# Differences of key groups with chained scores, a fifth block of maxima, a one-piece turn, and a list schedule for phase 1

## The chip, the cores and the metric

The kernel runs on one core of a Trainium2 chip. The metric is the device time of one execution in microseconds; lower is better.

## The reference

Attention over 8 batches and 8 heads with pairs of query rows pooled, and then a token and channel mixer on its output:

```
q_pool = q.reshape(B, H, S // 2, 2, D).mean(axis=3)       # S = 1152, D = 64
scores = scale * (q_pool @ k.T)                           # 576 x 1152 per head
scores = scores - max(scores, axis=-1)
attn = exp(scores);  attn = attn / (sum(attn, -1) + 1e-9)
x = attn @ v                                              # 576 x 64 per head, heads side by side: 576 x 512
theta = x @ w_theta;  zr = x * cos(theta);  zi = x * sin(theta)
y = w_tok_r @ zr + w_tok_i @ zi                           # over the 576 tokens
u = x + y;  out = u + relu(u @ w_ch)
```

q, k and w_theta come with large values, so the float32 scores are formed as a sum of products of high and low parts.

## The kernel before

**Phase 1, attention.** The 64 heads are worked two at a time: 32 pairs, one head in partitions 0 to 63 and one in 64 to 127. For each pair SyncE's queue loads q and k (`load_q`, `load_k`, four DMAs each) and v. VectorE pools the queries (`pool_q`, L291) and turns queries and keys in two pieces into PSUM (`prep_t`, tiles pt, L320 and L322). ScalarE rounds them to `hi` (`prep_hi`, L348), VectorE subtracts to get `lo` (`prep_lo`, L359).

The maximum of each query's scores comes from hi products alone. `maxpass` makes 12 tiles `pm` (4 blocks of 128 queries, 3 groups of 384 keys; one TensorE matmul a head, L374), and VectorE reduces each (`mx`, L381). 576 queries are 4.5 blocks; the half block left over is done for both heads at once by `max_tail`, with a block-diagonal operand `tail` (copied by ScalarE, L355), four wider matmuls into `px` and `py` (L391, L395) and two reductions (L396, L397). `max_nm` joins and negates them and turns the result with four 32 by 32 transposes (L403) into `nt`; `load_max` carries it by four small DMAs into a row `nmr` of minus maxima.

The scores come in 18 tiles a pair (`escore`: 2 halves of the queries, 9 tiles of 128 keys). A tile is the sum of four terms in PSUM (hi by hi, hi by lo, lo by hi, and a row of ones by `nmr`), each one matmul a head, 8 in all (L429). ScalarE takes the exponential out of PSUM into an SBUF tile `pc` (L432; 14 buffers). GpSimd adds tiles 0 to 6 of each half into `ss` (L442). TensorE multiplies each `pc` tile by v (`av`, L456) and sums the rest of the denominators with a matrix of ones (`norm_sum`, L478). The sums go out to DRAM and back in another layout (`rd`, `rc`), VectorE inverts them (L505), they go out and back again (`ro`, `dn`), and VectorE scales and turns the result (`norm_out` L527, `norm_turn` L532), which is stored in DRAM (`xd`, `xbd`).

Beside it run 18 jobs that rebuild the mixer's weights from 64-bit words (`weights`, L590 to L663), a step here and there on every engine. Those of the token weights end with a turn on TensorE (L656, L663; PSUM tile pwt). The jobs' SBUF pool is given back in `early`, after the last of them, and the first load of the attention's output for phase 2 (`xload`, xT, L182) goes into that space, so it waits for that last turn.

**Order.** Each step has a position (18 to a pair, from tables such as `MAX_AT`, `AV_AT`, `PREP_AT`, `PLAN`, and `PRO` for the first pairs); the list `todo` is sorted by it, and each engine runs its own steps in that order. av stands in runs of 9, 4 and 5 tiles. PSUM holds four slots of two banks; `bank2` gives the next tile the slot that a small cost model (`HOLD`) says comes free first. A tile of maxima or scores can so take any slot that is free.

**Phase 2, the mixer** (from L765 on) is not touched: batch by batch theta (L836), sines, the token mix (L924) and the channel mix (L963). It opens with xT cast into `xh` and `xl` (L193, L199), which theta reads.

## Time and profile before

| | before |
|---|---|
| median of 3 runs | 1284.25 us (1282.39 to 1284.72) |
| the profiled execution | span 1283.3 us from first to last instruction |
| start, up to the first score | 33.13 us |
| pairs 0 to 31, first score to first score | 774.51 us over 31 pairs, 24.98 us each |
| last pair's first score to the first theta | 27.8 us |
| phase 2, from 834 us to the end | 449 us |
| TensorE, VectorE, ScalarE, GpSimd busy, share of the span | 97%, 74%, 52%, 58% |
| the same in the middle of phase 1 (430 to 530 us) | 98%, 88%, 62%, 78% |
| TensorE's granted clock, mean | 0.988 |

The profile shows one execution. Engines run side by side and meet through semaphores; the share of busy time tells which is full, the timeline of an engine which instruction waited and for whom. The trace gives matmuls that overlap in the array, so their cost is read from start to start, not from the duration.

### The profile page before, as it was taken

The numbers are of one execution on the slowest core, as the hardware profiler recorded it, in microseconds if no ns is written. First come the engines' busy times: TensorE is split into PE (matmuls) and PEld (weight loads), VectorE is DVE, ScalarE is ACT, GpSimd is POOL, SyncE is SP. The second block draws the span as 40 slices with busy tenths as digits, with TensorE's granted clock in tenths as the row PEclk, the third lists the DMA queues.
The fourth block names the chain that finished last, engine by engine and source line by source line (L and its number), as shares of the span: only waits on it lengthen the run. The fifth ranks groups of instructions, "written<-read, shape, count | busy, mean of one in ns | idle before, by whom it ended". The sixth has DMA issues, their size and how long they took to land.

```text
span 1283.3 us, 29416 instructions
## 1 busy us (share of the span) xinstructions
...
## 2 busy tenths in 40 slices
...
GB/s 92 128 83 135 116 131 111 122 118 149 119 113 133 111 139 131 120 117 130 123 124 123 119 104 60 126 93 98 103 49 84 97 32 108 39 89 97 36 47 37
DMA packets 482235, 131.05 MB, mean 102 GB/s; under 512 B 451745, under 2 KB 452129, under 8 KB 482097
## 3 DMA queue, kind: packets, MB, share of 16 engines
...
q14 instruction: 48, 0.39, 0.1%
HBM read 97.21 MB, written 30.70 MB: 100 GB/s over the span
## 4 chain that ended last, share of the span: by engine, by line
PE 83%; DVE 8%; issue 3%; DMA 2%; POOL 2%; ACT 1%; SPq 0%; DVEq 0%; POOLq 0%; ACTq 0%
PE pa L456 20%; PE pe L429 19%; PE py L924 17%; PE pr L963 8%; PE pth L836 8%; PE pm L374 6%; DVE mx L381 4%; PE pns L478 3%; POOL ss L442 1%; DVE qk L291 1%; PE px L391 1%; DMA nmr<-nt 1%; DVE wf L599 1%; DVE mx L396 1%; DMA rc<-rd 1%
## 5 line engine op out<-in xcount | busy, mean ns | idle before, releaser
L442 POOL TENSOR_TENSOR ss<-ss,pc 128x576 f32<-128x576 f32 x314 | 463.5, 1476 | 52.5 <-ACT pc L432 32.2
L381 DVE TENSOR_REDUCE mx<-pm 128x2 f32<-128x768 f32 x384 | 357.0, 953 | 80.0 <-PE pm L374 77.9
L432 ACT ACTIVATE pc<-pe 128x576 f32<-128x576 f32 x576 | 349.8, 652 | 75.0 <-PE pe L429 61.7
L456 PE MATMUL pa<-pc,vn 128*64 128x288 f32 x2304 | 300.4, 410 | 0.4 <-ACT pc L432 0.4
L456 PEld LDWEIGHTS pa<-pc,vn 128*64 128x64 f32 x2304 | 156.9, 137 | 108.7 <-issue 5.7
L924 PE MATMUL py<-wtk,Z 128*128 128x288 f32 x1728 | 233.8, 296 | 0.0
L924 PEld LDWEIGHTS py<-wtk,Z 128*128 128x128 f32 x1728 | 232.3, 189 | 1.3
L897 POOL TENSOR_TENSOR Z<-ab,Z 128x512 fp32r<-128x512 f32 x40 | 52.1, 1303 | 258.8 <-ACT Z L893 251.8
L429 PE MATMUL pe<-hi 64*128 64x288 f32 x1152 | 182.0, 311 | 0.3 <-DVE lo L359 0.2
L429 PE MATMUL pe<-nmr,oner 64*128 64x288 f32 x1152 | 171.2, 292 | 0.0
L429 PE MATMUL pe<-lo,hi 64*128 64x288 f32 x1152 | 170.9, 292 | 0.0
L429 PE MATMUL pe<-hi,lo 64*128 64x288 f32 x1152 | 170.7, 292 | 0.0
L442 POOL TENSOR_TENSOR ss<-pc,pc 128x576 f32<-128x576 f32 x64 | 91.9, 1435 | 126.4 <-ACT pc L432 126.0
L374 PE MATMUL pm<-hi 64*128 64x384 f32 x768 | 145.7, 377 | 16.2 <-ACT hi L348 5.8
L429 PEld LDWEIGHTS pe<-hi 64*128 64x128 f32 x1152 | 109.3, 185 | 24.2 <-issue 7.5
L374 PEld LDWEIGHTS pm<-hi 64*128 64x128 f32 x768 | 73.2, 187 | 64.0 <-DVE mx L381 16.5
L348 ACT CAST hi<-pt 128x768 fp32r<-128x768 f32 x64 | 56.3, 879 | 114.2 <-DVE pt L320 105.3
L429 PEld LDWEIGHTS pe<-lo,hi 64*128 64x128 f32 x1152 | 109.9, 186 | 0.0
L429 PEld LDWEIGHTS pe<-hi,lo 64*128 64x128 f32 x1152 | 109.6, 186 | 0.0
L429 PEld LDWEIGHTS pe<-nmr,oner 64*128 64x128 f32 x1152 | 109.1, 185 | 0.0
L963 PEld LDWEIGHTS pr<-us,wch 128*128 128x128 f32 x768 | 104.2, 189 | 1.6
L963 PE MATMUL pr<-us,wch 128*128 128x288 f32 x768 | 105.2, 296 | 0.0
(101 smaller groups left out, 1426.8 us busy)
## 6 DMA issues: line engine op xcount, KB each, us to landing
...
xn<-xbd SPq DMA_DIRECT2D x140, 64.0 KB
```

Source lines behind the costliest of these rows:

```text
L348: nc.scalar.copy(hi, src)
L374: nc.tensor.matmul(pm[:, h, 0:W], hi[hs, Q0 + j * P : Q0 + (j + 1) * P], hi[hs, K0[3 * g] : K0[3 * g] + W], start=True, stop=True,)
L381: nc.vector.tensor_reduce(mx[:, j : j + 5 : 4, g : g + 1], pm[:, :, 0:W], AX.X, ALU.max)
L429: nc.tensor.matmul(pe[:, h, 0:HALF], w[hs], x[hs], start=(n == 0), stop=(n == 3))
L432: nc.scalar.activation(pcs[u, kt], pe[:, :, 0:HALF], AF.Exp, scale=SC)
L442: eng.tensor_tensor(st["ss", u], first, st["pc"][u, kt], ALU.add)
L456: nc.tensor.matmul(pa[hs, 0, 0:HALF], st["vn"][:, h, (kt + 3) % KT, :], st["pc"][u, kt][:, h, :], start=(kt == 0), stop=(kt == KT - 1),)
L478: nc.tensor.matmul(px[a : a + 32, 1, 0:HALF], ones, sets[u][n][:, h, :], start=(n == 0), stop=(n == len(sets[0]) - 1), tile_position=(0, a),)
L836: nc.tensor.matmul(th, xs[c][:, j * P : (j + 1) * P], ws[:, c], start=(n == 0), stop=(n == 11))
L897: engine("zlo", b).tensor_tensor(Z[1], t, Z[0].bitcast(F32), ALU.subtract)
L924: nc.tensor.matmul(st["py", c, u][:, 0:HALF], Z[zi][:, c * P : (c + 1) * P], wtk[wi][:, kw, u * HALF : (u + 1) * HALF], start=(i == 0 and ...
L963: nc.tensor.matmul(pr[u][:, 0:HALF], wch[wi][:, c, e * P : (e + 1) * P], st["us", ui][:, c, u * HALF : (u + 1) * HALF], start=(n == 0), st ...
```

## The change

Keys are replaced by differences. `load_k` brings the same keys; then two subtractions (`diff`, on GpSimd, on VectorE for the first pair) turn key groups 1 and 2 of 384 keys into their difference from the group before. A PSUM tile that has summed the product with group 0 and then with the difference of group 1 holds the scores of group 1. The score tiles stand in six chains a pair of three tiles (`CHAINS`: half, tile in the group, step): the first tile of a chain (`op.acq`) has all four terms, the next two have three terms, add to the same banks, and go in only after the exponential has read what stood there. Maxima chain in the same way over the three key groups of a block, behind their reduction. The half block of queries becomes a fifth block (`QB = 5`) with an overlapping set of 128 queries, and `max_tail`, `tail`, `px` and `py` go. The minus maxima are turned by one transpose over all partitions, still in 32 by 32 blocks, and loaded by six DMAs.

The order and the PSUM slots of phase 1 come from `operations` (every step with its engine, its needs and a position from `PLACE`) and `schedule` (a list scheduler, which lets an engine take a step ahead of another only at the first two pairs and the last). The weight jobs are placed `wd` positions apart. av runs are no longer cut by `AV_AT`. The names of phase 2's steps move to other line numbers; its code stays.

```
+CHAINS = ((0, 0, 0), (0, 1, 0), (0, 0, 1), (0, 1, 1), (0, 0, 2), (0, 1, 2), (0, 2, 0), (1, 0, 0), (0, 2, 1), (1, 0, 1), (0, 2, 2), (1, 0, 2), (1, 1, 0), (1, 2, 0), (1, 1, 1), (1, 2, 1), (1, 1, 2), (1, 2, 2))
...
+    "ns50": 43.96992, "slack": 0.16717, "turn": 17.33779, "w0": -5.19739, "wd": 35.76329,
...
+QB = 5
...
+        def diff(op):
+            kn = state[op.i]["kn"]
+            c = (2 - op.a) * W
+            (nc.vector if op.eng == DVE else nc.gpsimd).tensor_tensor(
+                kn[:, c : c + W], kn[:, c : c + W], kn[:, c - W : c], ALU.subtract
+            )
+
...
-            st = state[i]
-            hi, tl, mx = st["hi"], st["tail"], st["mx"]
-            pm = bank2("px", f"px{i}")
-            for n, c, k, w in ((0, 0, 0, 4), (1, 0, 4, 2), (1, 2 * P, 6, 2)):
+            if "mx" not in st:
+                st["mx"] = sml.tile([P, 2 * QB, 3], F32, tag="mx", name=f"mx{i}")
+            return st["mx"]
+        def max_mm(op):
+            hi, j, g = state[op.i]["hi"], op.a, op.b
+            q = Q0 + min(j * P, SQ - P)
+            pm = slots[op.slot]
+            for h, hs in enumerate(HEADS):
                 nc.tensor.matmul(
-                    pm[:, n, c : c + w * P], tl, hi[:, K0[k] : K0[k] + w * P], start=True, stop=True
+                    pm[:, h, 0:W],
+                    hi[hs, q : q + P],
+                    hi[hs, group(g)],
+                    start=(g == 0),
+                    stop=True,
+                    skip_group_check=(g > 0),
                 )
-            py = bank2("py", f"py{i}")
-            nc.tensor.matmul(py[:, 0, 0:P], tl, hi[:, K0[8] : K0[8] + P], start=True, stop=True)
-            nc.vector.tensor_reduce(mx[:, 8, 0:2], pm, AX.X, ALU.max)
-            nc.vector.tensor_reduce(mx[:, 8, 2:3], py[:, 0, 0:P], AX.X, ALU.max)
-
-        def max_nm(i):
-            st = state[i]
-            nc.vector.tensor_reduce(nm[:, 0:KT], st["mx"], AX.X, ALU.max, negate=True)
-            for g in range(0, P, TB):
-                nc.vector.transpose(nt[:, g : g + TB], nm[g : g + TB])
-
-        def load_max(i):
+        def max_nm(op):
+            nc.vector.tensor_reduce(nm[:, 0 : 2 * QB], state[op.i]["mx"], AX.X, ALU.max, negate=True)
+
+        def max_turn(op):
+            nc.vector.transpose(nt, nm)
+
+        def load_max(op):
+            rows = nmrs[op.i % 2].bitcast(F32).rearrange("(h d) c -> h d c", h=2)[:, 0]
+            g = op.a
+            if g < 4:
+                dst = rows[:, 0 : 4 * P].rearrange("h (c g r) -> h c g r", c=4, g=4)[:, :, g]
+                src = nt[TB * g : TB * g + 8]
+            else:
+                n = g - 4
+                dst = rows[:, 4 * P + TB * n : 4 * P + TB * (n + 1)]
+                src = nt[TB * (2 + n) + 8 : TB * (2 + n) + 10]
+            nc.sync.dma_start(dst, src)
+
+        def escore(op):
+            st = state[op.i]
+            u, k = op.a, op.b
+            hi, lo, nmr = st["hi"], st["lo"], nmrs[op.i % 2]
...
-            terms = (
-                (hi[:, ks], hi[:, qs]),
-                (hi[:, ks], lo[:, qs]),
-                (lo[:, ks], hi[:, qs]),
-                (oner, nmr[:, us]),
-            )
+            terms = [(hi[:, ks], hi[:, qs]), (hi[:, ks], lo[:, qs]), (lo[:, ks], hi[:, qs])]
+            if op.acq:
+                terms.append((oner, nmr[:, us]))
             for n, (w, x) in enumerate(terms):
                 for h, hs in enumerate(HEADS):
                     nc.tensor.matmul(
-                        pe[:, h, 0:HALF], w[hs], x[hs], start=(n == 0), stop=(n == 3)
+                        pe[:, h, 0:HALF], w[hs], x[hs],
+                        start=bool(op.acq and n == 0), stop=(n == len(terms) - 1),
+                        skip_group_check=not op.acq,
                     )
-            nc.scalar.activation(pcs[u, kt], pe[:, :, 0:HALF], AF.Exp, scale=SC)
...
+    x0 = add(SP, 1.2, 5.0, "early", 0, "early", 0, list(last))
...
-        def early():
-            while not run(wgen, 20):
-                turn_next()
...
+        def early(op):
             pw.close()
...
             xload(0)
```

What stands on the engines in a row, at three places. First TensorE in the middle of phase 1, beside the same kind of work; pe is a score tile, pm a maxima tile, and in the kernel after both have the names of the four PSUM slots (b_101 to b_104, L780 scores, L730 maxima). Before:

```order
L429 MATMUL pe_03_11832<-hi_11012 128x288 x2
L429 MATMUL pe_03_11832<-lo_11013,hi_11012 128x288 x2
L429 MATMUL pe_03_11832<-hi_11012,lo_11013 128x288 x2
L429 MATMUL pe_03_11832<-nmr_116,oner 128x288 x2
L374 MATMUL pm_12_11842<-hi_11405 128x384 [waits DVE_49]
L374 MATMUL pm_12_11842<-hi_11405 128x384
L429 MATMUL pe_04_11847<-hi_11012 128x288 [waits Activation_49]
L429 MATMUL pe_04_11847<-hi_11012 128x288
L429 MATMUL pe_04_11847<-lo_11013,hi_11012 128x288 x2
L429 MATMUL pe_04_11847<-hi_11012,lo_11013 128x288 x2
L429 MATMUL pe_04_11847<-nmr_116,oner 128x288 x2
```

After:

```order
L780 MATMUL b_104<-hi_8285 128x288 [waits Activation_49]
L780 MATMUL b_104<-hi_8285 128x288
L780 MATMUL b_104<-lo_8286,hi_8285 128x288 x2
L780 MATMUL b_104<-hi_8285,lo_8286 128x288 x2
L780 MATMUL b_101<-hi_8285 128x288 [waits Activation_49]
L780 MATMUL b_101<-hi_8285 128x288
L780 MATMUL b_101<-lo_8286,hi_8285 128x288 x2
L780 MATMUL b_101<-hi_8285,lo_8286 128x288 x2
L780 MATMUL b_101<-nmr_120,oner 128x288 x2
L730 MATMUL b_102<-hi_8603 128x384 [waits DVE_49]
L730 MATMUL b_102<-hi_8603 128x384
L780 MATMUL b_104<-hi_8285 128x288 [waits Activation_49]
```

Before, each score tile has four terms and a tile of its own. After, the first tile here adds three terms to slot b_104 and waits for ScalarE, the second starts a chain in b_101 with four, and the third is b_104 again.

Second, the end of phase 1. VectorE before, from the last weight turn on (wtk), with rc the sums of the last pair but two:

```order
L527 TENSOR_TENSOR xu_11262<-xu_11262,dn_12038 128x576 [waits DMAHW7_49,DMAHW0_49]
L532 STREAM_TRANSPOSE xb_12197<-xu_11262 128x576 [waits DMAHW4_49,DVE_49]
L505 RECIPROCAL rc_12136<-rc_12136 128x9 [waits DMAHW1_49]
L193 CAST xh_12113<-xT_12112 128x640 [waits DMAHW7_49,DMAHW6_49,Pool_49]
L199 TENSOR_TENSOR xl_12117<-xT_12112,xh_12113 128x640 [waits DVE_49]
L193 CAST xh_12114<-xT_12112 128x640
L199 TENSOR_TENSOR xl_12118<-xT_12112,xh_12114 128x640 [waits DVE_49]
L193 CAST xh_12115<-xT_12112 128x640
L199 TENSOR_TENSOR xl_12119<-xT_12112,xh_12115 128x640 [waits DVE_49]
L193 CAST xh_12116<-xT_12112 128x640
```

VectorE after (L543 and L549 are the casts xh and xl, L849 the reciprocal, rc_10586 the last pair's sums):

```order
L1041 TENSOR_TENSOR wtk_79<-b_104,wtk_78 128x4x64 [waits PE_49,Activation_49]
L1041 TENSOR_TENSOR wtk_79<-b_104,wtk_78 64x64
L543 CAST xh_10575<-xT_10574 128x640 [waits DMAHW6_49,DMAHW7_49,DVE_49,Pool_49]
L543 CAST xh_10576<-xT_10574 128x640
L549 TENSOR_TENSOR xl_10579<-xT_10574,xh_10575 128x640 [waits DVE_49]
L849 RECIPROCAL rc_10586<-rc_10586 128x9 [waits DMAHW4_49]
L543 CAST xh_10578<-xT_10574 128x640
L549 TENSOR_TENSOR xl_10580<-xT_10574,xh_10576 128x640 [waits DVE_49]
L543 CAST xh_10577<-xT_10574 128x640
L549 TENSOR_TENSOR xl_10581<-xT_10574,xh_10577 128x640 [waits DVE_49]
```

The reciprocal stood ahead of all the casts and was an earlier pair's; now it is the last pair's and stands behind two casts, ahead of the other two, xh_10578 and xh_10577. SyncE's queue there, before:

```order
L182 DMA xT_12112<-xd_82 128x4x576 [waits DVE_49,PE_49,DMAHW6_49,Activation_49,Pool_49]
L185 DMA xT_12112<-xd_83 128x4x64 [waits DMAHW7_49]
L299 DMA vn_12134<-in_v_dram 128x2x576 [waits DMAHW0_49]
L501 DMA rc_12136<-rd_12082 128x9 [waits DMAHW5_49,DMAHW1_49]
L541 DMA xd_89<-xu_11262 128x576 [waits DMAHW2_49,DVE_49]
L544 DMA xbd_97<-xb_12197 128x576 [waits DMAHW3_49,DVE_49]
L510 DMA ro_12297<-rc_12136 128x9 [waits DMAHW4_49,DVE_49]
```

and after:

```order
L532 DMA xT_10574<-xd_82 128x4x576 [waits DVE_49,PE_49,DMAHW6_49,Activation_49,Pool_49]
L535 DMA xT_10574<-xd_83 128x4x64
L839 DMA rd_10584<-sm_10568 4x288 [waits DMAHW0_49,Activation_49]
L1106 DMA x_10637<-xd_82 128x4x64 [waits PE_49]
L1106 DMA x_10637<-xd_82 128x4x64 [waits DMAHW2_49]
L532 DMA xT_10628<-xd_83 128x4x576 [waits DMAHW3_49]
L845 DMA rc_10586<-rd_10584 128x9 [waits DMAHW4_49,DMAHW0_49]
L854 DMA ro_10593<-rc_10586 128x9 [waits DMAHW5_49,DVE_49]
```

The load of xT stood ahead of the sums of three pairs; now it stands ahead of the last pair's alone, and three more loads (x, and the second xT) stand between the two halves of the last pair's way through DRAM (rd and rc). On TensorE (no rows) the last weight turn was followed by the whole last pair; after the change only six instructions, of av and the sums, stand between it and phase 2's first.

Third, the start of ScalarE (`hi` of the first pair is what the first maxima need). Before:

```order
L348 ACT_TABLE_LOAD
L348 CAST hi_140<-pt_0_142 128x768 [waits PE_49]
L348 CAST hi_140<-pt_0_154 128x960 [waits PE_49]
L355 CAST tail_120<-pt_0_154 64x64 [waits DVE_49,Pool_49]
L355 CAST tail_120<-pt_0_154 64x64
```

After (L944 and L948 are steps of the first weight job, whose data SyncE's queue loads behind q, k and v of the first pair):

```order
L944 ACT_TABLE_LOAD [waits DMAHW5_49]
L944 ACTIVATE raw<-raw 128x513 [waits DMAHW4_49]
L713 CAST hi_172<-b_101 128x960 [waits PE_49]
L713 CAST hi_172<-b_102 128x768 [waits PE_49]
L948 ACTIVATE wf<-raw 128x3x171
```

A weight step that waits for that load now stands ahead of the first casts; and the two tail copies are gone.

## Rows read from the trace of the kernel before

**Rows 1.** Windows of the trace: stretch and its length, busy us of each engine, clock, DMA.

```profile
430.00:530.00 100.00, 98.48 (x1083) 72.18 (x1079) 88.39 (x121) 62.48 (x111) 77.94 (x55) 1.00 0.59 126
...
834.00:1283.00 449.00, 440.32 (x2976) 418.84 (x2968) 236.09 (x410) 181.50 (x298) 136.61 (x104) 0.99 0.37 72
```

**Rows 2.** Timeline of TensorE, one pair: start us, duration, line, operation, count, idle before.

```profile
430.70 0.73 PE L391 MATMUL px<-hi,tail 128*128 128x512 f32 x3 [0.29 <-DVE mx L381]
...
437.26 0.29 PE L429 MATMUL pe<-hi 64*128 64x288 f32 x2
...
437.66 0.29 PE L429 MATMUL pe<-nmr,oner 64*128 64x288 f32 x2
...
437.79 0.29 PE L429 MATMUL pe<-hi 64*128 64x288 f32 x2
...
440.07 0.34 PE L374 MATMUL pm<-hi 64*128 64x384 f32 x2
...
440.24 0.39 PE L429 MATMUL pe<-hi 64*128 64x288 f32 x2
...
447.10 4.59 PE L456 MATMUL pa<-pc,vn 128*64 128x288 f32 x36
...
451.62 0.40 PE L429 MATMUL pe<-hi 64*128 64x288 f32 x2
```

**Rows 3.** Groups by line and form, 230 to 690 us: count, busy us, mean ns, idle before.

```profile
L442 POOL TENSOR_TENSOR ss<-ss,pc 128x576 f32<-128x576 f32 x184 | 271.9, 1478 | 25.2 <-ACT pc L432 13.3
...
L381 DVE TENSOR_REDUCE mx<-pm 128x2 f32<-128x768 f32 x222 | 206.9, 953 | 47.5 <-PE pm L374 46.1
...
L291 DVE TENSOR_TENSOR qk<-qn 128x576 f32<-128x576 f32 x19 | 24.6, 1297 | 0.0
...
L396 DVE TENSOR_REDUCE mx<-px 128x2 f32<-128x1024 f32 x19 | 23.1, 1216 | 0.0
...
L403 DVE STREAM_TRANSPOSE nt<-nm 32x32 f32<-32x32 f32 x72 | 14.4, 200 | 1.4
```

**Rows 4.** Timeline of ScalarE and VectorE beside rows 2: an exponential, a maximum, a pool_q.

```profile
452.46 0.65 ACT L432 ACTIVATE pc<-pe 128x576 f32<-128x576 f32 x1 [0.32 <-PE pe L429]
...
440.45 0.96 DVE L381 TENSOR_REDUCE mx<-pm 128x2 f32<-128x768 f32 x1 [0.27 <-PE pm L374]
...
453.51 0.75 DVE L291 TENSOR_TENSOR qk<-qn 128x576 f32<-128x576 f32 x1
```

**Rows 5.** Timelines of the start: ScalarE and TensorE.

```profile
9.46 0.80 ACT L348 CAST hi<-pt 128x768 fp32r<-128x768 f32 x1 [7.43 <-PE pt L334]
...
33.13 0.44 PE L429 MATMUL pe<-hi 64*128 64x288 f32 x2
```

**Rows 6.** Timelines of the end of phase 1: TensorE, SyncE's queue, VectorE, TensorE.

```profile
804.82 0.22 PE L663 MATMUL pwt<-ident,ws 64*128 64x64 f32 x1
...
807.64 0.40 PE L429 MATMUL pe<-hi 64*128 64x288 f32 x2
...
805.17 0.38 SPq L182 DMA_DIRECT2D xT<-xd  x1
...
806.75 0.64 SPq L501 DMA_DIRECT2D rc<-rd  x1
...
814.05 0.22 DVE L505 RECIPROCAL rc<-rc 128x9 f32<-128x9 f32 x1 [5.32 <-DMA rc<-rd]
...
822.99 0.82 DVE L199 TENSOR_TENSOR xl<-xT,xh 128x640 fp32r<-128x640 f32 x1
...
823.73 0.48 DVE L193 CAST xh<-xT 128x640 fp32r<-128x640 f32 x1
...
835.44 2.11 PE L836 MATMUL pth<-wth,xh 128*128 128x512 f32 x8
```

**Rows 7.** Timeline of TensorE in phase 2, the same two instructions with and without idle before.

```profile
886.15 2.12 PE L836 MATMUL pth<-wth,xh 128*128 128x512 f32 x8
...
894.49 3.29 PE L836 MATMUL pth<-wth,xh 128*128 128x512 f32 x8 [2.10 <-DVE r L862]
```

1031 lines of the change are left out of this document (615 added, 416 removed), and 34 rows, old and new, of the table PLACE.

## The prediction

> **What bounds the kernel now.** I read first how busy the engines are by stretch, then the timeline of the fullest one, then the groups of the others, and last the two ends of phase 1. In the middle of phase 1 TensorE is busy 98.48 of 100 us, VectorE 88.39, GpSimd 77.94 and ScalarE 62.48, and phase 2 holds TensorE for 440.32 of its 449 us [rows 1]. So TensorE sets the time in both phases, and a delay between them is not made good later. The first score of pair 0 starts at 33.13 us [rows 5] and that of pair 31 at 807.64 [rows 6]: 774.51 us over 31 pairs, **24.98 us a pair**. What a pair costs is therefore read from TensorE's steps, start to start, and the other engines matter where they come near that period. The profiled execution's span, 1283.3 us, lies 0.95 under the median of the runs, 1284.25; I add changes to the span and the 0.95 at the end.
>
> **Scores, on TensorE.** The fourth term of a tile starts at 437.66 and the next tile at 437.79 [rows 2]: a term costs 0.13 us, a four-term tile 0.53 (437.26 to 437.79), a three-term tile 0.40. Twelve of a pair's 18 tiles lose a term: 12 x 0.13 = **-1.56 us** a pair, all on the path.
>
> **Maxima.** The tail's px group takes 0.73 us, py included but for its end [rows 2]: -0.72. Three more pm at 0.17 each (440.07 to 440.24) are +0.51. Together **-0.2**. VectorE loses the 1.216 us reduction of px and gains three of 206.9 / 222 = 0.93 [rows 3].
>
> **Order of av.** An av run from 447.10 to 451.62 is 36 instructions in 4.52, and the matmul behind it takes 0.40 instead of 0.29 [rows 2]. After the change av stands in four runs a pair (2, 13, 2 and 1 tiles) instead of three. One run more means two more changes of the tile shape; at 0.11 to 0.2 each that is 0.2 to 0.4, and I take **+0.3**, nearer to the row's 0.11 twice than to nothing, with a little for the drain of the last av.
>
> So far 24.98 - 1.56 - 0.21 + 0.3 = 23.5 us. That still holds the waits of before, 1.5% or 0.4 us a pair.
>
> **The wait that the change adds.** A chained tile may only start when ScalarE has read its predecessor in the same banks, so TensorE, which works in order, holds maxima, av and everything else behind it. The rows give the loop: the tile that starts at 451.62 is read from 452.46 on for 0.65 us [rows 2, 4]. That one has four terms and 0.11 of a shape change ahead; with three terms the reading starts some 0.13 + 0.11 earlier, so predecessor start to successor start is about 1.3 us (1.45 with four terms). In that time the order places the predecessor (0.40), a tile of a second chain (0.40 to 0.53) and about one pm (0.17): about 1.0. Where only two chains alternate, 0.3 to 0.4 is missing for every two tiles; six such places would be 2.1 us a pair. Where av, the sums or a third chain lie between, nothing is missing. Walking through one pair in the new order with these steps, I find two places with the whole gap and a few tenths elsewhere. Bounds 0 and 2.1; I take **+0.7**, nearer to nothing because av and the sums fill about 10 us of the pair.
>
> Maxima chain as well: pm at 440.07, its reduction at 440.45 for 0.96 [rows 2, 4], the next pm of the block after that, 1.4 us. Two blocks alternate on two slots, so this is VectorE's own rate, 15 x 0.93 = 14 us a pair, beside other work; it is in the next sum.
>
> **VectorE and GpSimd.** VectorE: 88.39% of 24.98 is 22.1; plus 3 x 0.93, less 1.216, less three of the four 0.200 us turns [rows 3] makes 23.05 (py's small reduction left in). GpSimd: 77.94% of 24.98 is 19.5; each difference is 384 wide where an ss of 576 takes 1.478 [rows 3], so by estimate 0.99, and two are +2.0: 21.4. Both stay under 24.2, VectorE at 95%, so I cost the differences and the fifth block at nothing; what hides them is TensorE, and without that cover VectorE's 23.05 would be the floor.
>
> The row of pool_q shows VectorE waiting: 1.297 us on average, but 0.75 in the instance at 453.51 [rows 3, 4]. The Trainium skill (SBUF — State Buffer, Who interferes with whom) says that VectorE and GpSimd share a port pair as an exclusive lock, which a VectorE instruction with two SBUF inputs needs while GpSimd reads SBUF, and that the second to come is blocked for the whole instruction. The trace agrees, with 0.55 us on pool_q. By the rule at its worst, pool_q and norm_out each waiting for a whole difference more, VectorE would come to 23.05 + 2.0 = 25.0 and the time to about 1300; by the row, scaled with GpSimd's share, under 0.1 us is added.
>
> **A pair: 23.5 + 0.7 = 24.2 us**, between 23.5 and 25.6. Over 31 pairs -24.2 us.
>
> **The start.** ScalarE's first casts stood at 9.46 us [rows 5]; q and k of pair 0 had landed and been turned by then. Now a weight step that needs its own load stands ahead of them, and that load follows v and nearly doubles the bytes. Doubling can cost no more than another 8 us and no less than nothing (the load is in by then); I take 4. The six loads of the maxima at 0.64 us an issue, the length of a small issue in [rows 6], add 1.3 over four. Three more reductions less px's add 1.6. Against this I set some 3 us, since the first pairs have their own order now and more of pair 1 is ready when pair 0's scores begin. **+4**, bounds 1 and 8.
>
> **The end of phase 1.** Before, the last weight turn starts at 804.82, the load of xT goes out at 805.17 behind it, and phase 2's first theta runs at 835.44, a whole pair later [rows 6]: the load was hidden by the last pair. Now that turn stands two steps from the end of phase 1. VectorE then needs xT, casts two pieces, waits at the last pair's reciprocal, and casts the third piece, which theta reads, behind it. The reciprocal's load was 7.3 us from its issue (806.75) to its use (814.05) behind xT and v [rows 6], VectorE idle for 5.32 of it. I call T the end of phase 1's matmuls, about 834.3, 1.1 before 835.44. The sums go out at T + 0.9, their way back is issued about 3 us later and, with a second xT of the same size ahead of it, lands at T + 9 (T + 6 if nothing is in its way, T + 11 with the full 7.3). Behind it stand the reciprocal (0.22), a cast (0.48), a subtraction (0.82) and the cast that theta waits for (0.48) [rows 6]: theta goes on at T + 11, not T + 1.1, which is +9.9. After an idle 2.10 us the same theta took 3.29 us instead of 2.12 [rows 7], and I add that 1.1. **+11**, bounds 4 and 16. The last pair itself saves its 12 terms and loses a good part to chains with no maxima between: -0.5.
>
> **Sum.** -24.2 + 4 - 0.5 + 11 = -9.7: span 1273.6, and with 0.95, **1274.5 us**. Most of the gain in the pairs is paid back at the two ends.
>
> **Rivals.**
> *The gain is realised whole.* Other work fills every chain's loop and the waits stay at 0.4: 23.5 us a pair, 31 x 0.7 = 21.7 less, **1253**. For it: av and the sums fill much of a pair, and ScalarE is only 62% busy. Against: TensorE works in order and has no spare step to put in.
> *Slower: chains wait.* If two chains alternate in most of the pair, waits come to 1.5 instead of 0.7: 25.0 us a pair, +24.8, **1299**. It decides from 24.98 - (31 x 0.78 - 9.7) / 31, that is from 24.51 us a pair or waits of 1.0. For it: the loop of 1.3 to 1.45 against about 1.0 of work, and an exponential that ScalarE starts late lengthens it further. Before, a tile could take any free slot. The Trainium skill (Perfetto Trace Analysis, Optimizing Tensor Performance, Matmuls) says that independent groups of matmuls should rotate through PSUM banks, so that one is read out while the next is formed; the chain does the opposite. By the rule alone all six places would wait, 25.6 us a pair and 1318; by the rows, a third chain and av cover most of them, and no run here shows it yet.
> *VectorE becomes the bound.* At 95% it runs in order behind loads (dn, the maxima's way), and every late one delays the reduction for which the next pm waits. With 1.5 us of such stops on 23.05 a pair takes 24.55: **1285**. For it: the pm of before already waited for reductions. Against: VectorE was idle 11.6% and that idleness moved freely.
> *The end costs nothing.* If the reciprocal's load lands before VectorE reaches it and xT is early, +2 instead of +11: **1265**. Against it stands the order, not a row.
>
> **How the numbers follow.** Forecast (1268 to 1283) 0.42, gain whole 0.15, free end 0.08, chains wait 0.22, VectorE 0.13. About 0.2%, 2.6 us, is what a measurement of this kernel can tell from no change. Faster: 0.37 of the forecast, 0.15 and 0.08, together 0.60. Slower: 0.19 of the chains and 0.09 of VectorE, 0.28. The rest, 0.12, is within. The range takes in both outer rivals' centres but not their far halves: 1250 to 1298.
>
> **What would show it.** Right: first scores about 24.2 us apart; TensorE waiting for ScalarE's pc at scores, 0.5 to 1 us a pair; the first score at about 37; a gap of about 10 us on TensorE at the end of phase 1, released by a cast, with VectorE waiting there for rc. Wrong: pairs at 23.6 or less or 24.6 or more; waits named after mx or dn instead of pc; xT's casts done when the last sums end; a first score before 34.

## The result, and the profile after

The changed kernel takes **1299.09 us** in the median of 4 runs, against 1284.49 for the kernel before on the same chip: 1.0111 times as long, with a 95% interval of 1.0094 to 1.0127. One of those four executions took 2951.19 us, as one of "four loads" below took 4324.77; both stand outside the ratios, and without it the median is 1298.55. The forecast was 1274.5, range 1250 to 1298. The profiled execution's span is 1297.9 us, 14.6 more than before's. The two traces, cut at the same four points, give:

| us | before | after | difference | predicted |
|---|---|---|---|---|
| start to the first score | 33.13 | 39.06 | +5.9 | +4 |
| first score of pair 0 to that of pair 31 | 774.51 | 769.01 | **-5.5** | **-24.2** |
| that score to the last sums of phase 1 | 26.38 | 26.10 | -0.3 | -0.5 |
| last sums to the first matmul of the token mix | 17.19 | 30.77 | +13.6 | +11 |
| from there to the end | 432.13 | 432.92 | +0.8 | 0 |

Both ends cost about what was forecast; the pairs gained 18.7 us less. A pair takes 24.81 us instead of 24.98. I split the pair from TensorE's timeline between 130 and 755 us: the distance from one matmul's start to the next, less the distance of two steps of those kinds where nothing is waited for, is a wait; the rest is work.

| us a pair | work | waits | before a score | before a pm | before px | before av | before the sums |
|---|---|---|---|---|---|---|---|
| before | 23.69 | 1.31 | 0.72 | 0.14 | 0.33 | 0.12 | 0 |
| after | 22.04 | 2.77 | 1.33 | **1.03** | - | 0.19 | 0.21 |

How much of a pair is called a wait depends on the distance that is taken as free of waits, by some tenths of a us; the changes depend on it less. TensorE's work fell by 1.65 and the wait before scores grew by 0.61, near the forecast (1.47 and 0.7). What I had put at nothing is the wait before the maxima: 0.9 us a pair more before pm. The px tiles were maxima too, and their 0.33 went with them, so the maxima's waits grew by 0.56 us a pair net, 17 us over 31 pairs, nearly the 18.7 that are missing. First the windows (columns as in [rows 1]): TensorE is busy 94.45 where it was 98.48, VectorE 88.67 (88.39 before) and GpSimd 83.48 (77.94).

```profile
430.00:530.00 100.00, 94.45 (x978) 64.94 (x976) 88.67 (x110) 58.34 (x98) 83.48 (x62) 1.00 0.55 123
...
834.00:865.00 31.00, 19.72 (x89) 15.12 (x82) 15.60 (x25) 10.17 (x17) 4.36 (x3) 0.78 0.36 117
```

The waits between 230 and 690 us (who waits, for whom, us in total, times, longest), first before, then after:

```profile
DVE mx L381 <- PE pm L374: 46.1, 86, 1.2
ACT pc L432 <- PE pe L429: 30.5, 67, 0.9
...
PEld px L391 <- DVE mx L381: 9.8, 16, 0.9
PEld pm L374 <- DVE mx L381: 8.9, 17, 0.8
```

```profile
PEld b L730 <- DVE mx L742: 30.4, 73, 1.5
POOL qk L659 <- DVE xu L869: 29.0, 6, 6.9
POOL qk L659 <- DMA qk<-in_k_dram: 26.7, 10, 7.4
DVE lo L717 <- ACT hi L713: 24.9, 29, 2.8
...
ACT pc L790 <- POOL ss L797: 18.3, 15, 2.9
PEld b L780 <- ACT pc L790: 16.6, 50, 0.7
```

Before, VectorE waited for pm tiles (46.1 us) far more than TensorE's weight loads for pm did for maxima (8.9, and those for px 9.8). After, TensorE's weight loads wait 30.4 us for maxima, GpSimd's differences wait 55.7 us, and ScalarE waits 18.3 us for GpSimd's sums. The view puts 29.0 of the 55.7 down to VectorE's multiplication by dn, but it names the semaphore that came last among several: in each of these waits over 0.3 us the last load of the keys lands within 0.25 us of the difference's start, so it is the keys that GpSimd waits for. The chain that ended last shows the same by engine, before and after:

```profile
PE 83%; DVE 8%; issue 3%; DMA 2%; POOL 2%; ACT 1%; SPq 0%; DVEq 0%; POOLq 0%; ACTq 0%
```

```profile
PE 60%; DVE 10%; POOL 7%; SPq 7%; DMA 6%; ACT 6%; issue 4%; DVEq 0%; POOLq 0%; ACTq 0%
```

**Where a pair stops.** Quiet pairs take 23.8 to 24.2 us. About half the pairs have a stop of 0.4 to 2.4 us more, at one of two places. **Place A** is the second pm behind the long av run. The timelines of GpSimd, ScalarE, VectorE and TensorE, around 510 us:

```profile
495.00 1.01 POOL L659 TENSOR_TENSOR qk<-qk 128x384 f32<-128x384 f32 x1 [5.00 <-DVE mx L742]
...
505.68 10.38 POOL L797 TENSOR_TENSOR ss<-ss,pc 128x576 f32<-128x576 f32 x7
...
505.76 0.65 ACT L790 ACTIVATE pc<-b 128x576 f32<-128x576 f32 x1 [2.92 <-POOL ss L797]
506.30 0.95 ACT L713 CAST hi<-b 128x960 fp32r<-128x960 f32 x1
...
507.29 1.16 DVE L717 TENSOR_TENSOR lo<-b,hi 128x960 fp32r<-128x960 f32 x1 [2.80 <-ACT hi L713]
508.36 0.98 DVE L684 STREAM_TRANSPOSE b<-qk 128x768 f32<-128x768 f32 x1
509.25 1.30 DVE L963 SCALAR_TENSOR_TENSOR wf<-raw,wf 128x576 uint32<-128x576 uint32 x1
510.48 0.94 DVE L717 TENSOR_TENSOR lo<-b,hi 128x768 fp32r<-128x768 f32 x1
...
511.48 0.44 PE L730 MATMUL b<-hi 64*128 64x384 f32 x2 [2.13 <-DVE lo L717]
```

GpSimd stood still for 5.00 us ahead of a difference, for keys whose load was issued at 489.58 and landed at 494.79 (the row names a reduction), and is behind with its sums. ScalarE's exponential waits 2.92 us for one of them; `hi` stands behind it on ScalarE, `lo` waits for `hi`, a weight step stands ahead of the second `lo`, and TensorE's pm, whose slot that `lo` must free, waits 2.13 us. **Place B** is a pm behind the sums (VectorE, GpSimd, TensorE):

```profile
418.08 0.76 DVE L869 TENSOR_TENSOR xu<-xu,dn 128x576 f32<-128x576 f32 x1 [1.56 <-DMA dn<-ro]
418.76 4.41 DVE L742 TENSOR_REDUCE mx<-b 128x2 f32<-128x768 f32 x5
...
418.97 0.99 POOL L659 TENSOR_TENSOR qk<-qk 128x384 f32<-128x384 f32 x1 [6.88 <-DVE xu L869]
...
419.77 0.44 PE L730 MATMUL b<-hi 64*128 64x384 f32 x2 [1.25 <-DVE mx L742]
```

VectorE stands at the multiplication until dn has landed, the five reductions behind it start late, and pm waits 1.25 us. Averaged over all pairs A costs 0.31 us and B 0.38, of which 0.13 stands at B in every pair, stop or not; 0.2 stands at one more pm in every pair. Dn is late by the new order: in the kernel before it had landed 14.5 us ahead of the multiplication (median of 22 pairs), now 0.1 us. SyncE's queue sends the inverted sums out (`ro`) 5.2 us after the reciprocal instead of 0.4, and asks for dn 1.2 us after `ro` has landed instead of at once.

**The end of phase 1** came as forecast (TensorE, SyncE's queue, VectorE; compare [rows 6]):

```profile
832.46 0.22 PE L1023 MATMUL b<-ident,ws 64*128 64x64 f32 x1
...
839.74 1.22 PE L1133 MATMUL pth<-wth,xh 128*128 128x512 f32 x2
848.10 2.93 PE L1133 MATMUL pth<-wth,xh 128*128 128x512 f32 x6 [7.14 <-DVE xh L543]
...
832.82 0.37 SPq L532 DMA_DIRECT2D xT<-xd  x1
...
837.02 0.51 SPq L532 DMA_DIRECT2D xT<-xd  x1
839.14 0.33 SPq L845 DMA_DIRECT2D rc<-rd  x1
...
839.19 0.90 DVE L543 CAST xh<-xT 128x640 fp32r<-128x640 f32 x2 [4.88 <-DMA xT<-xd]
...
845.01 0.21 DVE L849 RECIPROCAL rc<-rc 128x9 f32<-128x9 f32 x1 [4.19 <-DMA rc<-rd]
...
846.22 1.82 DVE L543 CAST xh<-xT 128x640 fp32r<-128x640 f32 x1
```

xT goes out behind the last weight turn; theta does two matmuls and then waits 7.14 us for the cast of the third piece, the last of the four casts, which stands behind the reciprocal and its load. That cast took 1.82 us instead of 0.48: GpSimd's subtraction for xl ran from 845.87 to 847.69, and the cast ended 0.35 us later. While TensorE waited 4.11 us for xT (to 838.62), its granted clock fell to 0.50, the 1.2 GHz level, at 837.8 us; it rose at 851.5, when TensorE had run on from 848.10. In the kernel before it was 1.00 all through these 31 us. At **the start** ScalarE waited 11.64 us for the weight job's load, and the casts came at 13.49 instead of 9.46 [rows 5]:

```profile
11.64 1.28 ACT L944 ACT_TABLE_LOAD   x1 [11.64 <-DMA raw<-in_moe_w_theta_dram]
...
13.49 1.64 ACT L713 CAST hi<-b 128x960 fp32r<-128x960 f32 x2
```

### The profile page after: what moved, and what is told of

The parts are those of the page before. It is cut to its first block, busy times and chain, and to the rows that moved or that the text cites. A ratio compares the mean times of both kernels' runs of the same rounds, so it can differ in the third digit from the quotient of the medians.

```text
span 1297.9 us, 27681 instructions
## 1 busy us (share of the span) xinstructions
PE 1229.5 (95%) x10929; PEld 957.3 (74%) x10929; DVE 958.6 (74%) x1311; ACT 665.2 (51%) x1098; POOL 804.6 (62%) x600
## 3 DMA queue, kind: packets, MB, share of 16 engines
q8 instruction: 86, 1.41, 0.5%
## 4 chain that ended last, share of the span: by engine, by line
PE 60%; DVE 10%; POOL 7%; SPq 7%; DMA 6%; ACT 6%; issue 4%; DVEq 0%; POOLq 0%; ACTq 0%
PE py L1221 16%; PE b L802 12%; PE b L780 11%; PE pr L1260 8%; PE pth L1133 7%; PE b L730 5%; POOL ss L797 5%; DVE mx L742 4%; SPq L635 3%; ACT pc L790 2%; PE b L823 2%; DMA dn<-ro 2%; DMA qk<-in_k_dram 2%; ACT hi L713 1%; DVE b L684 1%
## 5 line engine op out<-in xcount | busy, mean ns | idle before, releaser
L797 POOL TENSOR_TENSOR ss<-ss,pc 128x576 f32<-128x576 f32 x314 | 451.9, 1451 | 14.3 <-ACT pc L790 1.9
L742 DVE TENSOR_REDUCE mx<-b 128x2 f32<-128x768 f32 x480 | 433.4, 950 | 30.9 <-PE b L730 26.2
L790 ACT ACTIVATE pc<-b 128x576 f32<-128x576 f32 x576 | 356.2, 650 | 182.0 <-PE b L780 140.1
L802 PE MATMUL b<-pc,vn 128*64 128x288 f32 x2304 | 307.2, 412 | 0.5 <-ACT pc L790 0.5
L802 PEld LDWEIGHTS b<-pc,vn 128*64 128x64 f32 x2304 | 154.1, 136 | 113.4 <-issue 23.4
L730 PE MATMUL b<-hi 64*128 64x384 f32 x960 | 186.8, 397 | 30.1 <-DVE mx L742 16.7
L780 PE MATMUL b<-hi 64*128 64x288 f32 x1152 | 185.2, 318 | 5.1 <-ACT pc L790 2.0
L780 PE MATMUL b<-lo,hi 64*128 64x288 f32 x1152 | 170.6, 292 | 0.0
L780 PE MATMUL b<-hi,lo 64*128 64x288 f32 x1152 | 170.4, 291 | 0.0
L730 PEld LDWEIGHTS b<-hi 64*128 64x128 f32 x960 | 89.6, 188 | 109.1 <-DVE mx L742 57.3
L780 PEld LDWEIGHTS b<-hi 64*128 64x128 f32 x1152 | 108.6, 185 | 38.5 <-ACT pc L790 30.9
L780 PEld LDWEIGHTS b<-lo,hi 64*128 64x128 f32 x1152 | 109.0, 186 | 0.0
L780 PEld LDWEIGHTS b<-hi,lo 64*128 64x128 f32 x1152 | 108.9, 185 | 0.0
```

The source lines that it names most:

```text
L730: nc.tensor.matmul(pm[:, h, 0:W], hi[hs, q : q + P], hi[hs, group(g)], start=(g == 0), stop=True, skip_group_check=(g > 0),)
L742: nc.vector.tensor_reduce(maxima(op.i)[:, at, g : g + 1], slots[op.slot][:, :, 0:W], AX.X, ALU.max)
L780: nc.tensor.matmul(pe[:, h, 0:HALF], w[hs], x[hs], start=bool(op.acq and n == 0), stop=(n == len(terms) - 1), skip_group_check=not op.acq,)
L790: nc.scalar.activation(pc, slots[op.slot][:, :, 0:HALF], AF.Exp, scale=SC)
L797: nc.gpsimd.tensor_tensor(st["ss", u], first, st["pc"][u, k], ALU.add)
L802: nc.tensor.matmul(half(op)[hs, 0:HALF], st["vn"][:, h, key(u, k), :], st["pc"][u, k][:, h, :], start=(k == 0), stop=(k == KT - 1),)
```

## The experiments

All start from the changed kernel, but for one that starts from the kernel before. "Time" is the median and its ratio to the kernel before on the same chip, with the interval; "pair" and its waits are split as above; "gap" is from the last sums to the token mix. Executions of the changed kernel and its variants range over 2 to 8 us ("xT first" over 13), those of before over 1 to 4, so single effects are read from the trace's stretches and the time is their control. Each trace is of one execution, not always a typical one: those of "no dn", "xT first" and "three short" lie 2 to 6 us under their medians, that of "short exponentials" 4.6 over it.

| run | time, ratio | first score | pair | wait, score | wait, pm | A, B | gap |
|---|---|---|---|---|---|---|---|
| after | 1299.09, 1.0111 | 39.06 | 24.81 | 1.33 | 1.03 | 0.31, 0.38 | 30.77 |
| ends | 1296.64, 1.0084 [1.0058, 1.0110] | 35.30 | 25.09 | 1.37 | 1.17 | | 26.75 |
| no dn | 1300.73, 1.0127 [1.0103, 1.0152] | 39.27 | 24.75 | 1.34 | 0.91 | 0.46, 0.15 | 29.59 |
| short sign step | 1297.87, 1.0106 [1.0077, 1.0135] | 39.17 | 24.65 | 1.33 | 0.90 | 0.19, 0.39 | 29.57 |
| short differences | 1292.67, 1.0063 [1.0041, 1.0086] | 39.06 | 24.63 | 1.34 | 0.82 | 0.12, 0.38 | 29.89 |
| short maxima | 1298.40, 1.0114 [1.0099, 1.0130] | 37.36 | 25.03 | 1.35 | 1.17 | 0.39, 0.44 | 30.79 |
| zero term | 1330.52, 1.0365 [1.0348, 1.0382] | 38.93 | 25.76 | 1.44 | 0.44 | | 31.41 |
| before, three terms | 1271.75, 0.9905 [0.9890, 0.9920] | 33.07 | 24.66 | 1.22 | 0.35 | | 17.22 |
| few loads | 1290.26, 1.0048 [1.0033, 1.0063] | 40.24 | 24.44 | 1.34 | 0.65 | <0.06, 0.29 | 30.40 |
| short exponentials | 1290.29, 1.0052 [1.0034, 1.0069] | 39.16 | 24.80 | 1.01 | 1.41 | 0.08, 0.67 | 31.70 |
| xT first | 1284.82, 1.0008 [0.9992, 1.0024] | 35.47 | 24.71 | 1.34 | 0.88 | 0.26, 0.30 | 18.98 |
| four loads | 1301.02, 1.0121 [1.0104, 1.0139] | 40.40 | 24.66 | 1.34 | 0.89 | 0.26, 0.31 | 30.20 |
| mended | 1295.50, 1.0085 [1.0072, 1.0098] | 36.29 | 25.34 | 1.36 | 1.43 | 0.27, 0.33 | 18.97 |
| three short | 1287.09, 1.0020 [1.0011, 1.0028] | 39.39 | 24.31 | 1.35 | 0.49 | <0.06, 0.14 | 29.52 |
| four short | 1275.94, 0.9940 [0.9927, 0.9953] | 39.18 | 24.05 | 0.91 | 0.82 | <0.06, 0.13 | 30.86 |
| differences later | 1285.87, 1.0016 [1.0005, 1.0027] | 35.42 | 24.83 | 1.32 | 1.09 | 0.09, 0.63 | 18.98 |
| dn and differences later | 1312.92, 1.0219 [1.0204, 1.0235] | 35.23 | 26.06 | 1.60 | 1.97 | <0.06, 0.11 | 18.98 |
| dn ahead of lo | 1338.28, 1.0414 [1.0395, 1.0432] | 35.48 | 27.02 | 1.60 | 2.21 | 1.43, 0.13 | 18.99 |
| dn ahead of lo, differences later | 1307.40, 1.0168 [1.0150, 1.0185] | 35.02 | 25.94 | 1.48 | 1.72 | 1.08, 0.12 | 18.99 |

**The two ends.** "Ends" moves the weight step on ScalarE behind the first cast, and the last reciprocal behind the cast of xh's third piece:

```
+        sink(order, pick(order, "w_low", -1), pick(order, "hi", 0, 0))
+        sink(order, pick(order, "norm_recip", NPAIRS - 1), pick(order, "xhi", 0, 2))
```

> The kernel after with two steps moved, nothing else: the first weight job's step on ScalarE goes behind the first pair's two casts, and the last pair's reciprocal on VectorE goes behind xT's casts that theta reads. Theory (order at the two ends): the first score starts near 35 us instead of 39.06, the stop of TensorE at the end of phase 1 shrinks by about 5 us because the cast that theta waits for at 846.2 no longer stands behind the wait for rc; pairs unchanged at 24.8; in all about 9 us less, near 1290. Rival (the ends are set by transfers and by the clock, not by the order): first score still near 39, the first full theta still about 13 us after the last sums, time unchanged at 1299.

The first score came 3.8 us earlier and the gap shrank by 4.0, but the pairs took 5.7 us more, at the maxima again. "XT first" also gives xT its own SBUF space, allocated ahead of the weight jobs' pool, so that its load no longer waits for the last weight turn, and lifts it a pair:

```
+        xTs.append(xp0.tile([P, ND, 5 * P], F32, name="xT0"))
+        lift(order, pick(order, "early", 0), pick(order, "norm_spread", NPAIRS - 2))
+        sink(order, pick(order, "norm_recip", NPAIRS - 1), pick(order, "xlo", 0, 2))
```

> The kernel after with the start mended as in e1_ends, and at the end xT in SBUF space of its own, loaded ahead of the last pair's sums instead of behind the last weight turn; the casts xh stand in a row ahead of the subtractions, and the last reciprocal behind them. Theory (the end's 13.6 us are the late load, then the wait for rc): phase 2's first token mix starts about 18 us after the last sums instead of 30.8, and with the start 4 us earlier the time is near 1283. Rival (the gap is refilled by the last pair's own way through DRAM or by a slower clock): 25 us or more from the last sums to the token mix, time near 1290.

The gap fell to 18.98, 11.8 us less. Phase 2 (timeline of TensorE) starts after a wait of 0.93 us, and theta runs its eight matmuls in one, where after waited 7.14 us in the midst of them:

```profile
828.71 0.66 PE L1148 MATMUL pxn<-ident,xT 128*128 128x128 f32 x4 [0.93 <-ACT sm L858]
829.12 2.11 PE L1168 MATMUL pth<-wth,xh 128*128 128x512 f32 x8
```

The median is 14.3 us under the changed kernel's and equal to before's. Its 12 executions range from 1279.15 to 1292.51, and the trace is of the one at 1279.15. By the trace 15.4 of the 19.5 us that the two ends had cost came back; the pairs still give next to nothing.

**The terms.** "Zero term" gives the chained tiles a fourth term (ones by a tile of zeros); "before, three terms" leaves the fourth term out of 12 of 18 tiles in the kernel before, whose results then miss the minus maxima there:

```
-            if op.acq:
-                terms.append((oner, nmr[:, us]))
+            terms.append((oner, nmr[:, us]) if op.acq else (oner, zero))
```

> The kernel after, with a fourth term of zeros in the twelve chained tiles of a pair, so that TensorE has the 1.56 us a pair back that the chains saved. Theory A (TensorE still sets the pair): pairs from 24.8 to 26.3, 48 us more. Theory B (other engines and the queue set it): TensorE has waits to give, pairs to 25.2 to 25.6, 12 to 25 us more.

```
+            if kt % 3:
+                terms = terms[0:3]
```

> The kernel before, with the fourth term left out of twelve of a pair's 18 score tiles (the minus maxima are missing there), so TensorE has 1.56 us a pair less and nothing else is moved: no chain, no differences, no new order. Theory A (the term's price is wrong or it lies beside other work): pairs stay near 25, under 15 us less. Theory B (the saving is real where nothing else is added): pairs near 23.5, 45 us less. Between the two, other engines take over at that period.

Put back into the changed kernel, the 1.61 us of TensorE's work (23.65 less 22.04) cost 0.95 a pair: waits shrank by 0.66. Taken out of the kernel before, with its free slots, its order and no difference to make, 1.57 us of work (23.69 less 22.12) brought 0.34: TensorE's waits grew from 1.31 to 2.54 (at scores from 0.72 to 1.22, at pm from 0.14 to 0.35, the rest elsewhere). TensorE was the bound by little, and a lighter TensorE has to wait for other engines within 0.3 to 0.4 us a pair. That is the main finding, and it needs neither chains nor the new order; the places A and B, at which the changed kernel loses its time, do come with the new order.

**One suspect at a time.** The multiplication without dn (it multiplies xu by itself), the sign step of the weights on 48 of 576 columns (the expectation of the three doses, further down, says 1728), the differences on 32 of 384 columns, the reduction of the fifth block's maxima on 32 of 384:

```
-            nc.vector.tensor_tensor(st["xu"], st["xu"], st["dn"], ALU.mult)
+            nc.vector.tensor_tensor(st["xu"], st["xu"], st["xu"], ALU.mult)
```

> The kernel after, with norm_out multiplying by xu itself instead of dn, so that VectorE never waits there for the way through DRAM; the scaling by the sums is left out. Theory (VectorE's stops in order): VectorE idles 0.35 us a pair ahead of norm_out, and TensorE's stops of 0.4 to 1.5 us some 17 us into a pair vanish: pairs from 24.81 to about 24.4, 12 us less. Rival (TensorE waits for exponentials in every pair): pairs stay at 24.8. Rival (GpSimd's lag): stays at 24.7 to 24.8.

```
-                f, hi, 0xC0000000, f, ALU.bitwise_and, ALU.bitwise_or
+                f[:, :, 0:16], hi[:, :, 0:16], 0xC0000000, f[:, :, 0:16],
```

> The kernel after, with the weight jobs' sign step on VectorE done on 48 columns instead of 513 or 576, so that it takes about 0.2 us instead of 0.75 to 1.9; the rest of the weights' signs is left out. Theory (VectorE's stops in order): this step stands between the turn t0 and lo0 in the pairs that stop TensorE 7 to 10 us into a pair; with it short, 17 jobs give back about 1.1 us each, 15 to 19 us in all at most, 10 if half of it is covered. Rival (chain waits): no change, since quiet pairs have none of it. Rival (GpSimd's lag): up to 3 us.

```
-                kn[:, c : c + W], kn[:, c : c + W], kn[:, c - W : c], ALU.subtract
+                kn[:, c : c + 32], kn[:, c : c + 32], kn[:, c - W : c - W + 32], ALU.subtract
```

> The kernel after, with the two differences a pair made on 32 of their 384 columns, so that GpSimd has about 1.7 us less a pair; most of the difference is left out. Theory (GpSimd's lag: late sums hold pc buffers, ScalarE waits for a free one ahead of the cast hi, and VectorE and TensorE behind it): the waits of ScalarE for ss go (18.3 us in 460 now), the stops of more than 1 us with them, pairs near 24.2, 19 us less. Rival (VectorE's own stops, dn and the weight steps): under 5 us less. Rival (chain waits): no change.

```
+            w = W if j < 4 else 32
```

> The kernel after, with the three reductions of the fifth block of maxima made on 32 of 384 columns, which leaves out most of that block's maximum; TensorE's matmuls for it stay. It takes about 2.2 us a pair off VectorE and shortens three of the loops of a maxima tile. Theory (VectorE is the engine whose fullness couples the others): pairs from 24.8 to 24.0 or less, 25 us or more. Rival (SyncE's queue and the transfers behind it): pairs stay above 24.5. Rival (TensorE's chain waits): the block's own loops shorten by 0.7 each but the score chains stay, pairs near 24.4.

By the period of the negated maxima they gave 0.05, 0.11, 0.20 and nothing (24.77 to 24.72, 24.66, 24.57 and 24.91). The two readings of a pair differ by up to 0.12 (25.03 and 24.91 with short maxima), so effects under 0.1 are not told from nothing; in time no dn gave nothing (1300.73). Without dn place B fell from 0.38 to 0.15 and A rose to 0.46. Of these four the differences gave most, at place A, though GpSimd stands on no direct wait of TensorE. The fifth block's reductions gave nothing though they are VectorE's largest new load: VectorE's total is not the bound, the places at which its row meets TensorE's are.

**Loads and exponentials.** "Few loads" leaves out three of four loads of q and of k from pair 4 on (later pairs then use old data, and all share one buffer of q and one of k); "short exponentials" works on 144 of 288 columns:

```
+            if i > 3 and n > 0:
+                return
```

> The kernel after, with three of the four loads of q and three of the four of k left out from the fifth pair on (the data of the fourth pair stay in place), so that SyncE's queue issues 6 of some 21 transfers a pair less, 0.65 to 0.7 us each, and moves 864 KB less. Theory (SyncE's queue, issuing without a pause for 15 us a pair, makes dn and the keys late): the waits for dn and for the keys go, pairs near 24.2, 18 us less. Rival (VectorE's and GpSimd's own fullness): pairs stay at 24.6 or more.

```
-            nc.scalar.activation(pc, slots[op.slot][:, :, 0:HALF], AF.Exp, scale=SC)
+            nc.scalar.activation(pc[:, :, 0:144], slots[op.slot][:, :, 0:144], AF.Exp, scale=SC)
```

> The kernel after, with the exponential made on 144 of a tile's 288 columns a head into 14 buffers that were zeroed at the start, which leaves out half of the exponentials; order, slots and all other work as they are. An exponential gets about 0.2 us shorter, and so does every loop score, exponential, next score of a chain. Theory (the chains' loops set the quiet pairs' 24.0 us): about six exposed loops a pair give 0.2 each, pairs from 24.8 to about 23.6, 35 us less. Rival (loads, GpSimd and VectorE set the pair): pairs stay at 24.5 or more, under 10 us less.

With a light queue place A is gone and pairs fall by 0.37. For dn this shows the queue: it is now asked for 0.03 us after `ro` has landed, and lands 3.8 us ahead of the multiplication. For the keys it does not tell the queue from the loads themselves, as three of four are gone. Place B keeps 0.29 although VectorE waits for dn in no pair. What is left is the length of the multiplication, here in two neighbouring pairs (VectorE of that run):

```profile
268.94 0.94 DVE L877 TENSOR_TENSOR xu<-xu,dn 128x576 f32<-128x576 f32 x1
...
292.93 1.81 DVE L877 TENSOR_TENSOR xu<-xu,dn 128x576 f32<-128x576 f32 x1
```

In 19 of 25 pairs it took 0.92 to 0.95 us and TensorE's wait at B was 0.13; in the other six a weight job's step (`hl` or `wth`) had just begun on GpSimd, it took 1.81 and the wait was 0.83 or 0.84.

With short exponentials the scores' wait fell by 0.32 and the pm's rose by 0.38: by the trace, what the scores give back, the maxima take. The median, 8.8 us under the changed kernel's, says that some of it is kept.

**The one-piece turn.** Four turns and four loads of the maxima instead of one and six; "mended" has this, xT first, and the sign step behind the first lo:

```
-            nc.vector.transpose(nt, nm)
+            for g in range(0, P, TB):
+                nc.vector.transpose(nt[:, g : g + TB], nm[g : g + TB])
```

> The kernel after with one part undone: the minus maxima are turned by four 32 by 32 transposes and loaded by four transfers, as before. VectorE gets 0.6 us a pair more, SyncE's queue two issues of 0.6 us less. Theory (the queue makes dn and the keys late): 3 to 6 us less. Rival (VectorE's fullness): 5 us more or no change.

> e10_xT_first and e11_four_loads together, and the weight jobs' sign step moved behind lo0 where it stood between the turn t0 and lo0. Theory (sum of the parts): 1283 less 4 for the loads less 3 for the sign step, near 1276, under the kernel before. Rival (the stops mask one another, as e2 and e3 showed): no better than e10_xT_first.

The turn is worth nothing either way in a pair (24.66 against 24.81, but 1301.02 against 1299.09). The moved sign step stops a later maximum in many pairs (0.46 us a pair at a place that had none) and costs what the rest had won.

**Several at once.** The three doses (dn, sign, differences), and the exponential besides:

> The changed kernel with three steps shortened at once: the multiplication of the unnormalised output by dn takes no dn (it multiplies by the output itself, so it waits for no load), the sign step works on 48 of 1728 columns, and each difference on 32 of 384. Singly they gave back 0.09, 0.11 and 0.24 us a pair, 0.44 together. Theory (the stops mask one another, each shows where another is taken away): TensorE's wait at the maxima falls from 1.03 to about 0.3 us a pair, pairs take 24.1 to 24.2, and the time is about 1281, some 18 us under the changed kernel. Rival (something else holds the maxima, and single doses simply add): pairs at 24.4, the wait at the maxima at 0.6 or more, 1287 or above.

> The three doses of the run with three shortened steps, and each exponential on half of its columns besides. Theory (the chains' wait for ScalarE is a cause of its own, and in the run with the exponential alone the wait only moved on to the maxima): now that the maxima are held by nothing, it falls too; TensorE's wait at scores goes from 1.3 to 1.0 or less, pairs take 23.6 to 23.8 and the time is about 1270. Rival (TensorE is paced by VectorE's total work, so that what is gained at scores is lost at the maxima again): pairs stay at 24.1 or above and the wait at the maxima is 0.6 or more, 1280.

Three doses gave 0.50 us a pair (0.47 by the period), where the single ones come to 0.40 (0.36; the expectation put them at 0.44): by the traces the stops add, and little of them was masked. The times lean the other way: by their ratios the single doses come to 5 us and the three together to 12, at the edge of the noise, so whether the stops mask one another is not settled. Place A is gone, B is at 0.14, and pairs take 24.31, near the 24.2 that I forecast without any stops. With the exponentials too, scores wait 0.44 less and maxima 0.33 more: the rival's reading, at a time between the two (1275.94).

**The real order.** On "xT first": the differences two sums later on GpSimd; the multiplication two reductions later besides; and the multiplication out of the row of maxima, ahead of the first lo, its turn ahead of the second, without and with later differences:

```
+            part = pick(order, "diff", i, a)
+            near = [o for o in order[order.index(part) :] if o.name == "ss"]
+            sink(order, part, near[1])
```

> Nothing left out: the changed kernel with its xT loaded a pair earlier, and each difference of keys moved behind two further scale-and-sum steps on GpSimd, so that GpSimd waits less for the keys. Theory (GpSimd's wait for the keys, 3.5 us a pair by the trace, delays the sums behind it and with them the weight step on VectorE): the stops at the second maximum after the long av run go, 0.1 to 0.2 us a pair, and the time is 3 to 6 us under the kernel with the earlier xT alone. Rival (GpSimd's idle time is slack, or the stop moves to the multiplication behind dn): within 2 us of it.

```
+            norm = pick(order, "norm_out", i)
+            near = [o for o in order[order.index(norm) :] if o.name == "mx"]
+            sink(order, norm, near[1])
```

> Nothing left out: the changed kernel with its xT loaded a pair earlier, the differences of keys two scale-and-sum steps later, and the multiplication by dn two reductions of the maxima later in VectorE's row. Theory (the two stops at the maxima trigger in turn, and both must be moved at once): TensorE's wait at the maxima falls from 0.9 to 0.5 us a pair or less, pairs take 24.2 to 24.4 instead of 24.65, and the time is 8 to 14 us under the kernel with the earlier xT alone, about 1274 to 1277, faster than before by 0.6 to 0.8%. Rival (another cause holds the maxima): within 3 us of it.

```
+            norm, turn = pick(order, "norm_out", i), pick(order, "norm_turn", i)
+            sink(order, norm, pick(order, "norm_recip", i + 1))
+            sink(order, turn, pick(order, "t", i + 4, 0))
```

> Nothing left out: the changed kernel with its xT loaded a pair earlier, and the multiplication by dn taken out of the row of the maxima: it stands behind the next pair's reciprocal, ahead of the first lo, where VectorE waits 0.9 to 1.3 us for ScalarE, and its turn ahead of the second lo. Theory (the row of the maxima has no place for 0.8 to 1.5 us of other work, whether dn is late or not): the stop at the maximum behind the sums goes from 0.30 to about 0.12 us a pair, the one behind the long av run grows by at most 0.1, and the time is 2 to 6 us under the kernel with the earlier xT alone. Rival (lo is then late instead): the stop behind the long av run grows by 0.3 or more, and the time is the same or up to 5 us longer.

> Nothing left out: the multiplication by dn out of the row of the maxima, and the differences of keys two scale-and-sum steps later besides. Theory: both stops are then away, 0.1 to 0.2 us each a pair instead of 0.26 and 0.30, pairs take 24.3 to 24.4 instead of 24.65, and the time is 1274 to 1278, faster than before by 0.5 to 0.8%. Rival (lo becomes late behind the multiplication in every pair): pairs at 24.65 or above, 1284 or more.

Later differences do empty place A (0.09), and B takes it (0.63). Moved by two reductions, the multiplication waits for nothing but stops TensorE there in every pair, by 1.53 us. VectorE, GpSimd and TensorE of that run, then a later pair's multiplication with GpSimd idle from 533.68 to 537.31:

```profile
509.60 1.41 POOL L821 TENSOR_TENSOR ss<-ss,pc 128x576 f32<-128x576 f32 x1
...
509.70 1.93 DVE L893 TENSOR_TENSOR xu<-xu,dn 128x576 f32<-128x576 f32 x1
...
512.55 0.44 PE L754 MATMUL b<-hi 64*128 64x384 f32 x2 [1.88 <-DVE mx L766]
...
535.58 0.75 DVE L893 TENSOR_TENSOR xu<-xu,dn 128x576 f32<-128x576 f32 x1
...
537.31 1.01 POOL L683 TENSOR_TENSOR qk<-qk 128x384 f32<-128x384 f32 x1 [3.62 <-ACT pc L814]
```

Ahead of `lo`, where VectorE waited 0.9 to 1.3 us for ScalarE, it empties place B (0.13, as in a pair without a stop) as the theory said, and A rises to 1.43, as the rival said. There it takes 1.93 us as well (VectorE and TensorE of that run):

```profile
500.81 1.93 DVE L893 TENSOR_TENSOR xu<-xu,dn 128x576 f32<-128x576 f32 x1
503.69 1.16 DVE L741 TENSOR_TENSOR lo<-b,hi 128x960 fp32r<-128x960 f32 x1 [0.95 <-ACT hi L737]
...
507.63 0.44 PE L754 MATMUL b<-hi 64*128 64x384 f32 x2 [1.06 <-DVE lo L741]
```

No place that I tried takes 0.8 to 1.9 us of other work on VectorE without a stop. None of these orders beats the kernel before; xT first equals it.

## Why the prediction was wrong

**Scores, maxima, order of av** (-1.47 on TensorE): right, -1.65 measured.

**The chains' wait** (+0.7): the size is right, +0.61 at scores, the cause only in part shown. With short exponentials 0.32 of the scores' wait goes, so ScalarE is in it; but the kernel before with three terms has no chains, and its scores wait 0.50 more as well. The rule on rotating PSUM banks (the Trainium skill, Perfetto Trace Analysis, Optimizing Tensor Performance, Matmuls) points the right way, but its price here is 0.61 us at most, not the 2.1 of all places waiting. The rival *Slower: chains wait* names nearly the measured time, 1299, by luck: it wanted 1.5 us of added wait at the scores.

**VectorE and GpSimd "at nothing": this step failed.** It asked whether their busy time stays under 24.2 us, and it does: in the windows above VectorE is busy 88.67 and GpSimd 83.48 of 100 us. But each runs in order, behind loads and behind each other, and TensorE meets VectorE's row at 15 maxima a pair and GpSimd's through `hi` and `lo`. The cover named, TensorE, was the thing being shortened, and the 14.5 us by which dn had come early, which the new order took, stood in no term. The waits at pm came to 1.03 us a pair, 0.9 more (0.56 net of px), two thirds of the 1.03 at A (GpSimd late for want of keys, then ScalarE, VectorE, TensorE) and B (VectorE behind dn). *VectorE becomes the bound* comes nearest in mechanism (reductions late behind dn, 24.55 a pair forecast, 24.81 measured), but cutting VectorE's total work did not help, and GpSimd, which it doesn't name, gave the largest effect of the four single steps. The lock's share, put at under 0.1 us, fell elsewhere: pool_q and the multiplication, which I had named, got no longer (1.31 to 1.25 and 0.85 to 0.79 us on average), the sign step did (0.94 to 1.59). My test of it, busy share, could not have shown that; the kernel before with three terms could: a saving on TensorE of 1.57 is worth 0.34 there.

**The waits of before** were carried over as 0.4 us, from a busy share of 98.48; split from start to start they were 1.31. A busy share counts a matmul's modelled end, and the short waits vanish in it. The sum does not depend on this, but the rival of the whole gain did.

**The start** (+4) measured +5.9, the casts' delay being the 4.0 and the maxima's way the rest: with short maxima the first score came 1.7 earlier. Of the 3 us that I had set against these some 1 came, if the loads cost the 1.3 that I gave them. **The end** (+11) measured +13.6, by the mechanism and the cast I had named; the load of the sums took 5.9 us from its issue (839.14 to 845.01), and the third piece's cast 1.82 instead of 0.48. Of the miss of 24.6 us the pairs make 18.7, the ends 4.5, the rest is small.

What is still open: of the 1.03 us before pm, 0.69 is placed at A and B and 0.18 at one more pm, and the wait at scores is not split by cause. Why pairs alternate between a quiet one and a stop was not settled, and whether some other list order reaches the 24.3 of the three doses was not found.
